# A chunked attention scan and two feed-forward layers on one core: a mask's row of 512 bytes, one raw load moved up, weight pieces fetched between other loads

## The chip, the cores and the metric

The kernel runs on one core of a Trainium2 chip. The metric is the device time of one execution in microseconds (us); the median of three runs of the kernel before is 595.84 us, with 594.42 the lowest and 600.78 the highest.

## The reference

Three layers follow one another on 3072 tokens (4 batches of 768) of 256 features. The first is a linear-recurrence attention with 8 heads, head size 32 and state size 16; the second squares a rectified product; the third multiplies two products. All of it is float32.

```python
def _attn_ref(x, a, B, C):
    log_a = np.log(np.clip(a, 1e-06, 1.0))
    state = np.zeros((batch, H, N, D), dtype=np.float32)
    for c in range(nc):
        xc, Bc, Cc, la = (chunk c of x, B, C, log_a)
        cum = np.cumsum(la, axis=-1)
        L = np.exp(cum[:, :, :, None] - cum[:, :, None, :]) * causal
        CB = np.einsum('bhin,bhjn->bhij', Cc, Bc)
        y_intra = np.einsum('bhij,bhjd->bhid', CB * L, xc)
        y_inter = np.einsum('bhin,bhnd->bhid', Cc, state) * np.exp(cum)[:, :, :, None]
        y[:, :, sl] = y_intra + y_inter
        state = decayed state + np.sum(Bx, axis=2)

def _moe_ref(x, w_in, w_out):        # 256 -> 2048 -> 256
    r = np.maximum(x @ w_in, 0.0)
    return r * r @ w_out

def _moe2_ref(x, w1, w2, w3, w_out): # 256 -> 1024 -> 1024 -> 256
    return ((x @ w1) * (x @ w2) @ w3) @ w_out
```

## The kernel before

**Tiles of tokens and phases.** The tokens go through in six tiles of 512. For a tile, phase A makes `h = x @ w_in` in 16 steps of 128 features (`h_mm`, line 700), rectifies it on ScalarE (line 712), squares it, and adds `g @ w_out` into two PSUM banks (`x2_mm`, line 745). Phase B makes the two products of the third layer in 8 steps (`a_mm` and `b_mm`, line 700 again), multiplies them and adds the product with `w3 @ w_out` into the output (`out_mm`, line 793). Each float32 operand of these products is split in a high and a low part of type fp32r (lines 142 and 139), and three matmuls stand for one product. The order is A0, A1, B0, B1, A2, B2 and so on to B5. `w3 @ w_out` itself is made once (`w3_product`, line 252).

**Attention.** The sequence is cut in chunks of 96 tokens, two of them to a unit. The first six chunks (units 0 to 2) are done in `startup`, ahead of phase A0. The later ones are spread over the phases as numbered slots: `unit_load` fetches a unit's raw B and C (tile `raw`), `unit_split` splits them and writes them to DRAM (`hl_d`), `unit_bc` reads them back in another shape (`bt`, `cb`, twelve small transfers), `unit_e` fetches decay rows (`e`), `chunk_xb` fetches x and B rows (`xb`), and `chunk_g`, `chunk_y` and `chunk_out` compute. Unit 5 is split in a slot of phase A0 (`put(ph, 7, unit_split, 5)`).

**Weights.** They arrive as 512 KB pieces of 8-byte words (tiles `ua`, `uo`, `u`), in an order fixed by `PIECES`: 16 for phase A (`ua0` to `ua15`), then others. `conv_load(n)` issues the next n of them. Each piece is rebuilt as float32 by ScalarE (lines 194, 196, 225) and VectorE (205, 208, 139); one piece goes with each step of phase A0.

**Order.** All transfers are issued by SyncE in the order in which the code is written (`dma` keeps the program's order), one queue, and each waits there for its inputs and for the transfer eight places ahead of it. In `startup` and A0 every engine keeps the written order as well (`in_order`, `held`).

**Addresses.** Tiles are laid out pool by pool. In the built program the weight tiles (pool `wts`) and the tiles `x20` and `x21`, which hold phase B's `x`, begin 320 bytes past a multiple of 512. Then comes `cmask`, 96 floats or 384 bytes in a row. Everything laid out behind it (`xt`, the moving operand of phase A's `h_mm`; `wo2`, in the same place; `tmp`, `gp`, and the attention's tiles) begins 192 past one, except that `xt` of tile 1 lies in the weight pool, at 320. `const` tiles (`bt`, `cb` of most units) begin at 128.

```python
    cmask = act1.tile([P, CH], F32, tag="cmask", name="cmask")
...
        chunk_xb(2)
        conv_load(1)
        for g in range(3, FIRST[1]):
            chunk_xb(g, f"w12{1 + g}")
        conv_load(2)
        unit_load(4)
...
        decays_e_out()
        conv_load(4)
```

Of the kernel before, what the change touches and what calls it, by code (L numbers as in the profile page):

```python
# [7 lines left out]
F32 = mybir.dt.float32  # L8
# [7 lines left out]
P = 128  # L16
# [3 lines left out]
CH = 96  # L20
# [36 lines left out]
def kernel(  # L57
# [102 lines left out]
    def conv_load(n=1):  # L160
        for _ in range(n):
            i = next_load[0]
            if i >= n_conv:
                return
            kind, j = PIECES[i]
            if kind == "3":
                if at_piece[0] <= last_in.get(PLACE[j % 8], -1):
                    return
                last_in[PLACE[j % 8]] = i + 2 - j % 2
                t = wts.tile([P, 512, 2], U32, tag=PLACE[j % 8], name=f"u3{j}")  # L170
                k = N_O + j
            else:
                place = f"w{kind}{j}"
                if at_piece[0] <= last_in.get(place, -1):
                    return
                t = wts.tile([P, 512, 2], U32, tag=place, name=f"u{kind}{j}")
                k = {"a": N_O + N_3, "o": 0, "12": N_O + N_3 + N_A}[kind] + j
            next_load[0] += 1
            dma(out=t, in_=w_in[k].bitcast(U32).rearrange("p (c w) -> p c w", w=2))
            stage[i] = t  # L180
# [88 lines left out]
    cb = const.tile([96, 4, 2, UW], F32R, name="cb")  # L269
    idc = const.tile([P, 4, 32], F32, name="idc")  # L270
    id2 = const.tile([P, 32], F32, name="id2")
    cmask = act1.tile([P, CH], F32, tag="cmask", name="cmask")
    ident = wts.tile([P, P], F32, tag="wa9", name="ident")
    e_d = dram.tile([4, 2, 2, 8, H, CH], F32, name="e_d")
    m_rel = new_tmp()
# [123 lines left out]
    def unit_load(u):  # L399
        gs = UNITS[u]  # L400
        n = len(gs) * CH
        raw = at.tile([P, 2, UW], F32, tag="raw", name="raw")
        b, t = divmod(gs[0] * CH, S)
        t0 = t
        while t < t0 + n:
            k, i = divmod(t, UT)
            m = min(UT - i, t0 + n - t)
            dma(
                out=raw[:, :, t - t0:t - t0 + m],
                in_=raw_in[b * (S // UT) + k].rearrange("p (s t) -> p s t", s=2)[:, :, i:i + m],  # L410
            )
            t += m
        units[u] = {"B": raw[:, 0, :n], "C": raw[:, 1, :n]}
# [56 lines left out]
    def unit_bc(u, places=None):  # L470
        n = len(UNITS[u])
        bu, cu = bt, [cb[:, :, pos] for pos in range(2)]
        units[u]["c2"] = None if places else cb
        if places:
            bu = wts.tile([96, 4, 2, P], F32R, tag=places[0], name="bt")
            cu = [wts.tile([96, 4, UW], F32R, tag=p, name="cb") for p in places[1:]]
            for c in cu:
                nc.gpsimd.memset(c.bitcast(F32), 0.0)
            unit_rows(bu)
        units[u]["bc"] = bu, cu  # L480
        hl = units[u]["hl"].rearrange("l (p r) s t -> l r p s t", p=4)
        for j in range(n):
            for k, part in enumerate((0, 0, 1)):
                dma(out=bu[32 * k:32 * k + 32, :, j, :CH].bitcast(F32), in_=hl[part, :, :, 0, j * CH:(j + 1) * CH])
        for k, part in enumerate((0, 1, 0)):
            for pos in range(2):
                r0 = 32 * k + 16 * pos
                dma(out=cu[pos][r0:r0 + 16, :, :n * CH].bitcast(F32), in_=hl[part, 16 * pos:16 * pos + 16, :, 1, :n * CH])
# [327 lines left out]
    def put(ph, s, f, *args):  # L816
        plan.setdefault((ph, s), []).append(lambda: f(*args))
# [83 lines left out]
    def attention_plan_1():  # L901
        ph = ("A", 0)
        for j, s in enumerate(ASLOT):
            g = FIRST[1] + j
            put(ph, s, chunk_pre, g)
            put(ph, s, chunk_mask, g)
            put(ph, s + 1, chunk_g, g, 0)
            put(ph, s + 1, chunk_g, g, 1)
            put(ph, s + 2, chunk_y, g)
        put(ph, 7, unit_split, 5)  # L910
        put(ph, 10, unit_bc, 5)
        put(ph, 12, unit_e, 5)
        put(ph, ASLOT[0] + 3, chunk_xb, 9)
        put(ph, ASLOT[1] + 3, chunk_xb, 10)
        put(ph, 2, unit_load, 5)

    def startup():
        ys = {}
# [14 lines left out]
        conv_load(1)  # L933
        chunk_xb(1)
        chunk_xb(2)
        conv_load(1)
        for g in range(3, FIRST[1]):
            chunk_xb(g, f"w12{1 + g}")
        conv_load(2)
        unit_load(4)  # L940
        for u in range(3):
            unit_e0(u)
        decays_ln()
# [13 lines left out]
        decays_e(1)  # L957
        unit_pad(2)
        decays_e_out()
        conv_load(4)  # L960
        chunk_pre(0)
        unit_gm(0, 0)
        unit_gm(0, 1)
# [12 lines left out]
        unit_split(3, "w120")  # L976
        unit_rows(bt)
        nc.gpsimd.memset(cb.bitcast(F32), 0.0)
        unit_bc(3)
        chunk_pick(1, 1)  # L980
        chunk_ds(1, ds[1])
# [13 lines left out]
        chunk_out(0, ys[0])  # L995
        chunk_hand(2, ds[2])
        chunk_xb(6)
        chunk_pick(3, 0)
        chunk_m0(2, 1)
        conv_bits(0)  # L1000
# [4 lines left out]
        chunk_m0(3, 0)  # L1005
        chunk_out(1, ys[1])
        unit_split(4, "w121")
        unit_e(3)
        chunk_xb(7)
        chunk_hand(3, ds[3])  # L1010
        chunk_pick(4, 0)
        conv_words(1)
# [11 lines left out]
        chunk_pick(5, 0)  # L1024
        chunk_m0(4, 1)
        chunk_out(3, ys[3])
        unit_bc(4, BCPLACE)
        unit_e(4)
        conv_bits(1)
# [22 lines left out]
    with in_order():  # L1052
        startup()
# [136 lines left out]
```

## Time and profile before

| | |
|---|---|
| median of 3 runs | 595.84 us (594.42 to 600.78) |
| the profiled execution | 599.25 us, of which the profile's span is 597.5 us |
| mean granted TensorE clock | 0.983 of full speed |
| TensorE matmul busy (PE) | 564.8 us, 95% |
| TensorE weight load busy (PEld) | 463.9 us, 78% |
| VectorE (DVE) | 345.4 us, 58% |
| ScalarE (ACT) | 308.1 us, 52% |
| GpSimd (POOL) | 90.5 us, 15% |
| moved by DMA | 60.33 MB, 101 GB/s over the span |

The shares are over the whole span, whose stages differ: the first 126 us hold the startup, the rebuilding of the weights and most of the waits; behind them TensorE has hardly an idle microsecond. The granted clock of a stretch is given as a share of full speed: 1.00 is 2.4 GHz and 0.50 is 1.2 GHz.

### The profile page before, as it was taken

How to read it: one execution, taken by the hardware profiler on the slowest of the kernel's cores; microseconds unless marked ns; L12 is line 12 of the kernel's file. 1: busy time of each engine (PE TensorE's matmuls, PEld its weight loads, DVE VectorE, ACT ScalarE, POOL GpSimd, SP SyncE). 2: the span in 40 equal slices, each digit the busy share in tenths (PEclk: the TensorE clock that was granted, in tenths of full speed). 3: DMA queues.
4: the chain of work that ended last, by engine and by line, in shares of the span. 5: the costliest groups of instructions: out<-in, count | busy, mean ns of one | idle time of the engine just before them, and what ended most of it. 6: DMA issues, size and time to landing. Idle time of an engine off the chain costs nothing.

```text
span 597.5 us, 10302 instructions
## 1 busy us (share of the span) xinstructions
PE 564.8 (95%) x3884; PEld 463.9 (78%) x3884; DVE 345.4 (58%) x613; ACT 308.1 (52%) x640; POOL 90.5 (15%) x149
## 2 busy tenths in 40 slices
PE   5776898899999999999999999999999999999997
PEld 5654676678888888888778888778888778888786
DVE  1677888687879745455646456544456553544332
ACT  4676898687876434353434354353444343534331
POOL 2817110000002313003023004021030030000000
PEclk8899799799999999999999999999999999999999
DMA  8857657124165543046241064230162220100001
GB/s 239 282 136 207 211 217 281 35 79 169 70 210 143 144 101 89 1 132 152 67 110 54 23 159 110 50 86 3 34 180 68 70 50 1 36 1 0 1 1 36
DMA packets 48850, 60.33 MB, mean 101 GB/s; under 512 B 22944, under 2 KB 36640, under 8 KB 48800
## 3 DMA queue, kind: packets, MB, share of 16 engines
q1 hardware_dynamic: 48800, 59.67, 34.3%
q8 instruction: 31, 0.51, 0.4%
q14 instruction: 19, 0.16, 0.1%
HBM read 50.99 MB, written 8.65 MB: 100 GB/s over the span
## 4 chain that ended last, share of the span: by engine, by line
PE 83%; DMA 7%; SPq 4%; DVE 2%; ACT 2%; issue 1%; POOL 0%; POOLq 0%; ACTq 0%; DVEq 0%
PE mm L700 42%; PE acc L745 20%; PE acc L793 12%; PE mm L252 4%; SPq L91 4%; DMA raw<-in_raw_dram 2%; PE y L667 2%; PE g L555 2%; DMA e<-e_d 2%; DMA hl_d<-hl 1%; DMA uo<-in_w_dram 1%; DMA u<-in_w_dram 1%; PE g L576 1%; PE mm L604 1%; PE y L651 1%
## 5 line engine op out<-in xcount | busy, mean ns | idle before, releaser
L745 PE MATMUL acc<-gp,wa 128*128 128x512 f32 x576 | 152.3, 402 | 7.9 <-ACT gp L728 6.7
L700 PE MATMUL mm<-xt,wa 128*128 128x512 f32 x576 | 152.0, 401 | 4.3 <-DVE wa L139 2.1
L728 ACT CAST gp<-tmp 128x512 fp32r<-128x512 f32 x144 | 89.4, 621 | 112.8 <-DVE tmp L784 53.1
L139 DVE TENSOR_TENSOR gp<-tmp,gp 128x512 fp32r<-128x512 f32 x144 | 102.1, 709 | 76.0 <-ACT gp L728 75.8
L700 PE MATMUL mm<-x,w 128*128 128x512 f32 x576 | 143.6, 395 | 0.8 <-ACT x L142 0.4
L745 PEld LDWEIGHTS acc<-gp,wa 128*128 128x128 f32 x576 | 107.2, 190 | 35.1 <-ACT gp L728 8.4
L700 PEld LDWEIGHTS mm<-xt,wa 128*128 128x128 f32 x576 | 106.9, 191 | 30.2 <-DVE wa L139 4.2
L700 PEld LDWEIGHTS mm<-x,w 128*128 128x128 f32 x576 | 104.3, 188 | 22.5 <-ACT x L142 1.1
L712 ACT ACTIVATE tmp<-mm 128x512 f32<-128x512 f32 x96 | 57.3, 597 | 48.4 <-PE mm L700 47.7
L793 PEld LDWEIGHTS acc<-w3o,gp 128*128 128x128 f32 x576 | 75.9, 189 | 4.6
L793 PE MATMUL acc<-w3o,gp 128*128 128x256 f32 x576 | 78.9, 284 | 0.0
L784 DVE TENSOR_TENSOR tmp<-tmp,mm 128x512 f32<-128x512 f32 x48 | 32.8, 683 | 55.8 <-PE mm L700 43.3
L722 DVE TENSOR_TENSOR tmp<-tmp 128x512 f32<-128x512 f32 x64 | 45.0, 703 | 31.5 <-ACT tmp L712 30.9
L776 ACT COPY tmp<-mm 128x512 f32<-128x512 f32 x48 | 27.7, 586 | 42.1 <-PE mm L700 40.9
L493 POOL TENSOR_SCALAR_AFFINE_SELECT e<-e 96x768 f32<-96x768 f32 x26 | 28.2, 1100 | 130.3 <-DMA e<-e_d 115.0
L512 POOL TENSOR_TENSOR xb<-xb,dec 96x256 f32<-96x256 f32 x32 | 22.3, 697 | 120.6 <-DMA xb<-in_xb_dram 113.5
L561 DVE TENSOR_TENSOR e<-g,e 128x384 f32<-128x384 f32 x52 | 27.6, 551 | 16.6 <-PE g L555 9.9
L512 POOL TENSOR_TENSOR pb<-xb,dec 96x128 f32<-96x128 f32 x32 | 15.8, 493 | 84.3 <-PE y L651 84.1
L667 PE MATMUL y<-e,xb 128*32 128x96 f32 x512 | 23.0, 263 | 3.4 <-issue 2.2
L667 PEld LDWEIGHTS y<-e,xb 128*32 128x32 f32 x512 | 13.3, 113 | 15.5 <-issue 12.0
L512 POOL TENSOR_TENSOR pb<-idc,dec 32x128 f32<-32x128 f32 x32 | 15.7, 491 | 56.5 <-PE y L651 54.7
L252 PE MATMUL mm<-wo,w 128*128 128x256 f32 x128 | 23.5, 283 | 0.5 <-DVE w L139 0.3
(90 smaller groups left out, 471.6 us busy)
## 6 DMA issues: line engine op xcount, KB each, us to landing
u<-in_w_dram SPq DMA_DIRECT2D x24, 512.0 KB, 4.1
e<-e_d SPq DMA_DIRECT2D x44, 192.0 KB, 4.3
ua<-in_w_dram SPq DMA_DIRECT2D x16, 512.0 KB, 7.6
xb<-in_xb_dram SPq DMA_DIRECT2D x32, 192.0 KB, 4.0
bt<-hl_d SPq DMA_DIRECT2D x78, 48.0 KB, 2.0
hl_d<-gp SPq DMA_DIRECT2D x9, 384.0 KB, 4.1
cb<-hl_d SPq DMA_DIRECT2D x66, 48.0 KB, 2.0
out_dram<-tmp SPq DMA_DIRECT2D x12, 256.0 KB, 2.2
```

The costliest lines, as they stand in the source:

```text
L139: return nc.vector.tensor_tensor(out=lo, in0=src, in1=hi.bitcast(F32), op=ALU.subtract)
L252: nc.tensor.matmul(acc[:, :DM], v[:, l, e % 4 * P:(e % 4 + 1) * P], wo2[1 + e // 2][r][:, e % 2 * DM:(e % 2 + 1) * DM], start=(n == 0), st ...
L493: nc.gpsimd.affine_select(out=m, in_=m, pattern=[[0, m.shape[1]], [1, CH]], base=0, channel_multiplier=-1, compare_op=ALU.is_ge, fill=0.0,)
L512: nc.gpsimd.tensor_tensor(out=out, in0=v_in, in1=d.to_broadcast([r.stop - r.start, 4, 2, out.shape[3]]), op=ALU.mult)
L667: nc.tensor.matmul(ys[32 * q:32 * q + 32, hg], ch["xb"][:, 32 * h:32 * h + 32], es[g][:, h], start=True, stop=True, skip_group_check=True,)
L700: nc.tensor.matmul(ps, w[m][:, l, col + k * P:col + (k + 1) * P], rhs[k][:, r, :], start=((l, r, k) == (1, 0, 0)), stop=((l, r, k) == (0, ...
L712: nc.scalar.activation(r, ps, AF.Relu)
L722: nc.vector.tensor_tensor(out=g32, in0=r, in1=r, op=ALU.mult)
L728: nc.scalar.copy(g[:, 0, :], d[k])
L745: nc.tensor.matmul(acc["x2", t][e], wa[m][:, l, 256 + e * P:256 + (e + 1) * P], g[:, r, :], start=(m == 0 and n == 0), stop=(m == MF - 1 a ...
L784: nc.vector.tensor_tensor(out=p32, in0=prods[t, m], in1=ps, op=ALU.mult)
L793: nc.tensor.matmul(acc["o"][sub // 2][:, sub % 2, :], g[:, l, sub * P:(sub + 1) * P], w3o[m // 2][:, r, m % 2, :], start=(m == 0 and n == ...
```

## The change

It has three parts. The mask's tile is made 128 floats wide, of which the first 96 are used, so that the tiles behind it move by 128 bytes and begin 320 past a multiple of 512, as the weights do. The raw load of unit 5 leaves slot 2 of phase A0 and is issued in `startup`, behind the writes of the decay rows. The weight pieces 1 to 7, which were issued in `startup` as 1, 2 and 4 at three places, are issued at seven places: behind the early loads, and singly or in pairs between the transfers of units 3 and 4. Together with that, `chunk_xb(7)` is issued ahead of `unit_e(3)`.

```diff
-    cmask = act1.tile([P, CH], F32, tag="cmask", name="cmask")
+    cmask = act1.tile([P, P], F32, tag="cmask", name="cmask")[:, :CH]
...
-        put(ph, 2, unit_load, 5)
...
         chunk_xb(2)
-        conv_load(1)
         for g in range(3, FIRST[1]):
             chunk_xb(g, f"w12{1 + g}")
-        conv_load(2)
         unit_load(4)
+        conv_load(1)
...
         decays_e_out()
-        conv_load(4)
+        conv_load(1)
+        unit_load(5)
...
         nc.gpsimd.memset(cb.bitcast(F32), 0.0)
+        conv_load(1)
         unit_bc(3)
...
         chunk_xb(6)
+        conv_load(1)
...
         unit_split(4, "w121")
+        chunk_xb(7)
+        conv_load(2)
         unit_e(3)
-        chunk_xb(7)
...
+        conv_load(1)
         unit_bc(4, BCPLACE)
```

On SyncE's queue, from the loads of `startup` to unit 3's write (`hl_d3`) and read-back, this stands in a row before; `e_d` are the decay rows, `raw_154` is unit 4's raw load.

```order
L91 DMA ua2_150<-in_w_dram 128x1024
L91 DMA ua3_152<-in_w_dram 128x1024
L91 DMA raw_154<-in_raw_dram 128x2x192
L91 DMA e_d_96<-tmp_178 128x4x96
L91 DMA e_d_96<-tmp_248 128x4x96
L91 DMA ua4_255<-in_w_dram 128x1024
L91 DMA ua5_257<-in_w_dram 128x1024
L91 DMA ua6_259<-in_w_dram 128x1024
L91 DMA ua7_261<-in_w_dram 128x1024
L91 DMA hl_d3_368<-hl_363 128x2x384
L91 DMA bt_90<-hl_d3_368 32x4x96 x6
L91 DMA cb_91<-hl_d3_368 16x4x192 x6
```

And there now:

```order
L91 DMA raw_148<-in_raw_dram 128x2x192
L91 DMA ua1_150<-in_w_dram 128x1024
L91 DMA e_d_96<-tmp_174 128x4x96
L91 DMA e_d_96<-tmp_244 128x4x96
L91 DMA ua2_251<-in_w_dram 128x1024
L91 DMA raw_253<-in_raw_dram 128x2x64
L91 DMA raw_253<-in_raw_dram 128x2x32
L91 DMA hl_d3_361<-hl_356 128x2x384
L91 DMA ua3_366<-in_w_dram 128x1024
L91 DMA bt_90<-hl_d3_361 32x4x96 x6
L91 DMA cb_91<-hl_d3_361 16x4x192 x6
```

Ahead of the write of unit 3 stand three pieces (0, 1 and 2) where eight stood, and unit 5's two raw transfers (`raw_253`) have come in. Further on in the same queue, around the decay rows of unit 4 (`e_683`) and the pieces that phase A0 starts to load, this stood before:

```order
L91 DMA cb_666<-hl_d4_556 16x4x192
L91 DMA e_683<-e_d_96 32x2x768 x4
L91 DMA ua8_764<-in_w_dram 128x1024
L91 DMA ua9_766<-in_w_dram 128x1024
L91 DMA raw_780<-in_raw_dram 128x2x64
L91 DMA raw_780<-in_raw_dram 128x2x32
L91 DMA ua10_792<-in_w_dram 128x1024
```

From unit 3's read-back to unit 4's, this stands there now:

```order
L91 DMA xb_487<-in_xb_dram 96x512
L91 DMA ua4_489<-in_w_dram 128x1024
L91 DMA hl_d4_553<-hl_548 128x2x384
L91 DMA xb_555<-in_xb_dram 96x512
L91 DMA ua5_557<-in_w_dram 128x1024
L91 DMA ua6_559<-in_w_dram 128x1024
L91 DMA e_561<-e_d_96 32x2x768 x4
L91 DMA xb_605<-in_xb_dram 96x512
L91 DMA ua7_665<-in_w_dram 128x1024
L91 DMA bt_667<-hl_d4_553 32x4x96 x6
```

Pieces 4 to 7 have come in here, and behind them unit 4's decay rows are followed by pieces 8 to 12 with no raw load between. The orders of TensorE, VectorE and ScalarE are as before; on GpSimd one mask of chunk 6 stands some instructions later.

## Rows read from the trace of the kernel before

**Rows 1.** The page's first part: busy us, share of the span, instructions.
```profile
PE 564.8 (95%) x3884; PEld 463.9 (78%) x3884; DVE 345.4 (58%) x613; ACT 308.1 (52%) x640; POOL 90.5 (15%) x149
```

**Rows 2.** Busy us by stage: PE, PEld, DVE, ACT, POOL, granted clock, DMA share, GB/s.
```profile
54.00:62.00 8.00, 2.66 (x12) 1.53 (x10) 3.61 (x10) 1.98 (x8) 3.75 (x5) 1.00 1.01 320
62.00:69.00 7.00, 7.00 (x38) 5.06 (x39) 5.74 (x11) 7.00 (x15) 1.14 (x2) 0.52 0.72 225
69.00:100.00 31.00, 30.86 (x197) 24.18 (x196) 26.86 (x47) 28.85 (x64) 4.57 (x7) 1.00 0.68 260
126.00:597.00 471.00, 466.19 (x2801) 387.60 (x2800) 257.06 (x452) 213.34 (x425) 55.31 (x85) 1.00 0.28 77
```

**Rows 3.** ScalarE in order of time, 51 to 64 us: start, us, idle before, releaser.
```profile
51.73 0.67 ACT L194 ACTIVATE cvs<-ua 128x512 f32<-128x512 f32 x1
...
54.27 0.62 ACT L225 CAST wa<-cvs 128x512 fp32r<-128x512 f32 x1
60.92 0.44 ACT L142 CAST gp<-raw 128x96 fp32r<-128x96 f32 x2 [6.02 <-DMA raw<-in_raw_dram]
...
61.79 0.67 ACT L194 ACTIVATE cvs<-ua 128x512 f32<-128x512 f32 x1
```

**Rows 4.** TensorE in order of time, 54 to 62 us.
```profile
55.99 1.67 PE L700 MATMUL mm<-xt,wa 128*128 128x512 f32 x6 [1.06 <-DVE wa L139]
61.93 0.80 PE L745 MATMUL acc<-gp,wa 128*128 128x512 f32 x1 [4.28 <-ACT gp L728]
```

**Rows 5.** SyncE's issues in order of time, 18 to 62 us.
```profile
18.06 2.90 SPq L91 DMA_DIRECT2D ua<-in_w_dram  x4
22.00 0.38 SPq L91 DMA_DIRECT2D hl_d<-hl  x1
30.34 3.40 SPq L91 DMA_DIRECT2D bt<-hl_d  x6
...
52.80 0.89 SPq L91 DMA_DIRECT2D ua<-in_w_dram  x2
53.73 1.38 SPq L91 DMA_DIRECT2D raw<-in_raw_dram  x2
```

**Rows 6.** The chain that ended last, 18 to 62 us: start, us, what.
```profile
22.00 8.32 DMA hl_d<-hl
...
54.34 6.50 DMA raw<-in_raw_dram
```

**Rows 7.** DMA issues from 18 to 21.5 us: KB each, median us to landing.
```profile
ua<-in_w_dram SPq DMA_DIRECT2D x4, 512.0 KB, 8.2
```

**Rows 8.** The chain that ended last, behind 126 us: start, us, what, matmuls.
```profile
129.96 1.37 PE mm L700 x6
...
139.37 1.38 PE mm L700 x6
```

**Rows 9.** The same chain behind 505 us; phase A5 from 517.93, B4 and B5 around it.
```profile
505.26 2.75 PE mm L700 x12
...
517.93 4.20 PE mm L700 x18
522.12 4.20 PE acc L745 x18
...
587.71 5.78 PE acc L793 x48
```

**Rows 10.** TensorE groups by shape, 120 to 597 us: busy us, mean ns of one.
```profile
L745 PE MATMUL acc<-gp,wa 128*128 128x512 f32 x473 | 122.6, 397 | 1.2 <-DVE gp L139 1.2
...
L793 PE MATMUL acc<-w3o,gp 128*128 128x256 f32 x576 | 78.9, 284 | 0.0
L252 PE MATMUL mm<-wo,w 128*128 128x256 f32 x120 | 22.0, 282 | 0.3 <-DVE w L139 0.3
L252 PE MATMUL mm<-wo2l,w 128*128 128x256 f32 x60 | 16.9, 282 | 0.0
```

**Rows 11.** The same view, 200 to 597 us: the `xt` matmuls of phases A2 to A5.
```profile
L700 PE MATMUL mm<-xt,wa 128*128 128x512 f32 x384 | 99.5, 395 | 0.0
```

## The prediction

> **What bounds the kernel now.** The page's first part comes first: TensorE's matmuls are busy for 564.8 of 597.5 us [rows 1]. That alone says little, since matmuls overlap, so the next view is the table of busy time by stage [rows 2]. From 126 us to the end TensorE is busy in 466.19 of 471 us, and ScalarE and VectorE in about half of them: there the time is the number of matmuls by the distance from one to the next, and nothing but a shorter distance saves anything. Ahead of that, from 62 to 100 us, ScalarE (35.85 of 38 us) and TensorE (37.86 of 38) are both full, because each step of phase A0 rebuilds a weight piece on ScalarE. A hole in this stretch moves all that follows it. There is one: between 54 and 62 us TensorE works for 2.66 us and ScalarE for 1.98.
>
> The engines' timelines show what the hole is. ScalarE ends a piece at 54.89 (54.27 + 0.62), and its next instruction, unit 5's split, waits 6.02 us for the tile `raw` [rows 3]. The cast of `gp` stands behind it, and TensorE, which needs that `gp`, stays idle for 4.28 us up to 61.93 [rows 4]. SyncE issued the raw load at 53.73 [rows 5] and the second of its two transfers took 6.50 us [rows 6], at a DMA share of 1.01 with weight pieces in front. Right behind the hole the granted clock is 0.52 over 7 us [rows 2], the lower level of 1.2 GHz for nearly all of it, after 4.28 idle microseconds at the upper level of 2.4 GHz.
>
> **The raw load moved up.** It goes from behind piece 9 to behind piece 2. The work that it feeds stays at its place. By the new order ahead of it stand the early loads, three pieces, and the decay rows; where the queue was fullest a piece landed 8.2 us after its issue [rows 7]. At its new place it is issued well before the 18.06 us at which piece 4 was issued [rows 5], so it lands by some 26 us and is wanted at 54.89. The 6.02 us of ScalarE go.
>
> What is late next? I followed ScalarE's order past the split. Two casts and the `gp` cast take it to about 55.8, and then it wants piece 8 (line 194, at 61.79 before, 0.87 us behind the split [rows 3]). Piece 8 was issued at 52.80 and stood just ahead of the raw load, which landed at 60.84. Would piece 8 alone have held the engine up? With the old queue, by about as long as its landing passes 55.8, so the reordering of the queue decides.
>
> **Weight pieces between other loads.** The bytes are the same; only places change. Before, four pieces were issued at 18.06 to 20.96, and the write of unit 3 (`hl_d`) behind them took 8.32 us from 22.00 [rows 5, 6]. Its read-back, 12 small transfers that SyncE issues one by one, started only at 30.34, and everything behind it on that in-order queue stood. Now the write has no such four in front. I estimate it at 2 to 4 us, an end at about 24 us, and 6 us won for the queue. Pieces 4 to 7 come back in behind it: four issues of 0.44 us (0.89 for two in [rows 5]), or 1.8 us, and their bytes take part of the old slack. So piece 8 is issued some 4 us earlier, at about 48.8, and lands some 6.5 us later, as long as the raw load took behind the same queue [rows 6], at 55.3. That is when ScalarE wants it. Pieces 4 to 7 have room: the last, piece 7, is wanted by line 194 at 51.73 [rows 3]. At the worst landing time shown, 8.2 us, it must be issued by 43.5. The read-back's first six issues took 3.40 us [rows 5], so all twelve end at about 31, and eleven more of about 0.45 us put piece 7 at 36.
>
> So the worth of both moves together lies between TensorE's hole of 4.28 us and ScalarE's of 6.02. More than ScalarE's is possible only by 0.6, since ScalarE is full on both sides. TensorE is full behind the hole as well, but 7 us of that ran at a granted clock of 0.52 [rows 2], and without the hole I expect 1.00, as ahead of it. That can shorten TensorE's own path by up to 3.4 us, half of the 7, on top of its 4.28, and leaves ScalarE the limit. I take 5.4 us, the middle of 4.3 and 6.6. It lies wholly on the path: from 62 to 126 us the same engines do the same work earlier, the later loads hang on TensorE's and VectorE's progress and move along, and behind 126 us there is no gap to swallow it.
>
> **The mask's row.** It adds no instruction; one tile grows by 128 bytes. What it moves is where the operands begin. The trace holds both cases. Phase A5's `h_mm` reads `xt` at 192 against weights at 320: 18 matmuls in 4.20 us, 233.3 ns each; `x2_mm` with `gp` at 192 takes the same [rows 9]. Phase B's `x` lies at 320 like its weights: 12 in 2.75 us, 229.2 ns [rows 9]. The nearest control is phase A1, with the same weight tiles as A5 but its `xt` in the weight pool, at 320: six in 1.37 and 1.38 us, 228 to 230 ns [rows 8]. So like beginnings go with a distance shorter by 3 to 4 ns, and I take 4.1.
>
> Where it counts: 473 `x2_mm` matmuls behind 120 us [rows 10] and 384 `h_mm` ones of A2 to A5 [rows 11], together 857; times 4.1 ns this is 3.5 us. The 256-column matmuls also mix beginnings now: 576 of `out_mm`, whose stationary `gp` is at 192, and 180 of line 252 [rows 10], at 120.4 ns (48 in 5.78 us [rows 9]). No row shows them with like beginnings. From zero to the whole 4.1 ns they give 0 to 3.1 us; a loss is not excluded, and with the sign turned it would be as large. I take half, as for half the columns: 756 times 2.05 ns, 1.5 us. Ahead of 120 us ScalarE sets the pace, and the shorter distance is hidden.
>
> The Trainium skill's page "SBUF — State Buffer", section "Who interferes with whom", speaks against this part: it gives TensorE two independent read ports, one for the moving operand and one for the weight load, and says that TensorE never waits on anyone. By that, where two operands begin could not matter, this term would be zero and the sum only the first one; the rows of A1 and A5 disagree with it by 3 to 4 ns a matmul.
>
> **Sum.** 5.4 + 3.5 + 1.5 = 10.4 us. On the profiled execution of 599.25 us that gives 588.8. That execution is 3.4 us above the median, inside the spread of the three runs, so I take the difference to the median: 595.84 - 10.4 = 585.4 us, 1.7% faster. Within 1% of the median (5.96 us) this kernel's measurement can hardly be told from no change.
>
> **The rivals.**
> 1. *Alignment is worth nothing.* The 3 to 4 ns would come from which tiles are read, not from where they begin. For it: no tile is seen at both places in the same use. Against it: A1 and A5 have the same weights and the same three passes. Time: 595.84 - 5.4 = 590.4. The page's rule above gives just this time.
> 2. *The hole is filled by the next late load.* If the write of unit 3 is not much quicker, piece 8 lands at 60 us and ScalarE waits for it instead of for `raw`, for 4 to 5 us; or a piece among 4 to 7 is late by as much. For it: piece 8 was issued directly ahead of the raw load and the queue is in order. Against it: four pieces leave its front. What remains is the alignment: 595.84 - 5.0 = 590.8.
> 3. *Like beginnings are the dear case.* If operands that begin alike met in the memory in the uses that no row shows, or `xt` in its new place did, each of the 857 + 756 matmuls would lose what I count as a gain: 1613 times 4.1 ns, 6.6 us. With the hole gone that is 1.2 us slower, 597.0; with rival 2 as well, 602. It decides from 3.4 ns on, where 1613 matmuls eat up the 5.4 us. Against it: both kinds of row with like beginnings are the quicker ones.
> 4. *Nothing arrives*: rival 1 and rival 2 together, 595.8.
>
> **How the numbers follow.** The forecast has a chance of 0.50, rival 1 0.17, rival 2 0.18, rival 3 0.07, rival 4 0.08. The predicted time is the forecast's, 585.4. The range: low end from 6.6 us for the hole and 3.5 + 3.1 us for alignment, 595.84 - 13.2 = 582.6, less the 1.4 us by which the lowest of the three runs lies under the median, 581.2. The high end takes in rivals 1 and 2 and ends at 591.5; left out are rivals 3 and 4 and the tails. Faster by over 1% (589.9 or less) is nearly all of the forecast and a third of rivals 1 and 2, which lie at the bound: 0.61. Slower by over 1% is rival 3 with rival 2, and late pieces that I did not foresee: 0.06. The rest, 0.33, is within 1%.
>
> **What the changed profile would show.** The split of unit 5 follows line 225 on ScalarE with no wait, and TensorE's idle time of 4.28 us near 58 us is gone or under 1 us. The granted clock stays at 1.00 from 54 to 69 us. Unit 3's write takes under 4 us. Phase A5's runs of 18 read 4.13 us or so, and 48 of `out_mm` 5.7. If ScalarE waits there for `ua` instead, rival 2 holds; if runs of 18 still read 4.20, rival 1; if they read more, rival 3. A second low-clock stretch earlier than 62 us would mean that pieces 4 to 7 come late. The prediction is wrong above all if piece 8 lands after 57 us.

## The result and the profile after

The changed kernel takes 592.43 us, the median of 20 runs (588.86 to 598.69). The kernel before, run beside it, takes 597.5 us (20 runs, 594.42 to 603.97). The ratio is 0.990 with a 95% interval of 0.987 to 0.993. It is formed from the undisturbed executions alone, so it isn't quite the quotient of the two medians. The forecast was 585.4 us with a range of 581.2 to 591.5: the kernel is faster, but by 1.0% and not by 1.7%, and the time lies 0.9 us above the range. The base moved as well: the forecast was taken off a median of 595.84 from three runs, and 20 runs give 597.5.

The profiled execution after has a span of 592.0 us, 5.5 less than before. Its stages, to be read against [rows 2] (PE, PEld, DVE, ACT, POOL, granted clock, DMA share, GB/s):

```profile
54.00:62.00 8.00, 4.96 (x41) 3.50 (x42) 3.58 (x10) 3.71 (x8) 2.14 (x4) 0.93 0.98 346
62.00:69.00 7.00, 7.00 (x24) 5.71 (x24) 6.88 (x14) 7.00 (x16) 1.86 (x2) 0.59 0.64 201
```

The hole is smaller, but it is there: between 54 and 62 us TensorE is busy for 4.96 us, and behind it the granted clock is again near its lower level of 1.2 GHz (0.59, before 0.52). ScalarE in order of time answers to [rows 3]:

```profile
52.84 0.44 ACT L142 CAST gp<-raw 128x96 fp32r<-128x96 f32 x2
53.19 0.61 ACT L728 CAST gp<-tmp 128x512 fp32r<-128x512 f32 x1
58.28 0.66 ACT L194 ACTIVATE cvs<-ua 128x512 f32<-128x512 f32 x1 [4.49 <-DMA ua<-in_w_dram]
```

The split of unit 5 has no wait, as forecast. Two instructions later ScalarE waits 4.49 us for piece 8. TensorE's stop, to be read against [rows 4], went from 4.28 us to 3.04. A `gp` cast of line 728 releases it again, but the next one in order, at 60.89; the cast that ended the stop before now runs at 53.19, ahead of the wait.

```profile
61.56 2.08 PE L745 MATMUL acc<-gp,wa 128*128 128x512 f32 x4 [3.04 <-ACT gp L728]
```

SyncE's issues say when piece 8 was asked for. The row at 52.80 begins with it, and answers to the one of the same start in [rows 5]:

```profile
20.13 0.37 SPq L91 DMA_DIRECT2D hl_d<-hl  x1
...
22.84 3.77 SPq L91 DMA_DIRECT2D bt<-hl_d  x6
...
40.91 6.39 SPq L91 DMA_DIRECT2D bt<-hl_d  x6
47.40 3.46 SPq L91 DMA_DIRECT2D cb<-hl_d  x6
50.97 1.77 SPq L91 DMA_DIRECT2D e<-e_d  x4
52.80 2.83 SPq L91 DMA_DIRECT2D ua<-in_w_dram  x5
```

Unit 3's write is issued at 20.13 and its read-back begins at 22.84 (before 22.00 and 30.34), so the queue did win 7.5 us. Unit 4's read-back begins at 40.91, where it began at 42.01, and piece 8 is issued at 52.80 in both. The first two of its twelve transfers go out at 40.91 and 43.94, each 0.02 us behind the landing of the piece eight places ahead (pieces 5 and 6, at 40.89 and 43.92). The chain that ended last shows what took the rest of the 7.5 us (start, us, what):

```profile
38.59 10.03 DMA ua<-in_w_dram
...
48.69 0.30 SPq L91
...
52.80 5.46 DMA ua<-in_w_dram
58.28 0.66 ACT cvs L194
```

Before, the same chain had decay rows at this place, landed at 47.29:

```profile
40.52 6.77 DMA e<-e_d
```

The piece issued at 38.59 is piece 7, for which the forecast had 36. It landed at 48.62, and SyncE's next issue in the chain follows 0.07 us later. By the queue's rule that each transfer waits for the one eight places ahead, that issue is the second `cb` of unit 4: behind piece 7 come six `bt` and one `cb`.

The alignment shows in phase A5, the runs of [rows 9] (and 36 matmuls of `w3_product`, which serve below as a mark of time):

```profile
127.50 4.31 PE mm L252 x36
...
513.66 4.11 PE mm L700 x18
517.76 4.08 PE acc L745 x18
...
582.16 5.76 PE acc L793 x48
```

Eighteen matmuls of 512 columns take 4.11 and 4.08 us where they took 4.20, so 228.3 and 226.7 ns each where it was 233.3. The 48 of 256 columns take 5.76 where they took 5.78: nothing. One new wait came up in phase B0. TensorE after, and below it the same place before:

```profile
201.45 0.39 PE L700 MATMUL mm<-x,w 128*128 128x512 f32 x1
203.56 0.66 PE L555 MATMUL g<-cb,bt 96*128 96x192 f32 x4 [1.72 <-DMA cb<-hl_d]
204.07 4.28 PE L700 MATMUL mm<-x,w 128*128 128x512 f32 x11
208.18 1.36 PE L793 MATMUL acc<-w3o,gp 128*128 128x256 f32 x10
```

```profile
205.76 0.39 PE L700 MATMUL mm<-x,w 128*128 128x512 f32 x1
...
206.72 2.73 PE L700 MATMUL mm<-x,w 128*128 128x512 f32 x11
209.29 1.37 PE L793 MATMUL acc<-w3o,gp 128*128 128x256 f32 x10
```

TensorE comes there 4.31 us sooner than before and leaves only 1.11 sooner: a wait of 1.72 us for a read-back that isn't there yet, then eleven matmuls at the lower clock, 4.28 us for 2.73. Where the 5.5 us of this execution arose, from the rows shown and those of before:

| mark on TensorE | before | after | gain so far |
|---|---|---|---|
| 36 matmuls of line 252, A1 | 131.33 | 127.50 | 3.83 |
| ahead of `cb`'s wait, B0 | 205.76 | 201.45 | 4.31 |
| ten matmuls of line 793 behind it | 209.29 | 208.18 | 1.11 |
| first run of 18, A5 | 517.93 | 513.66 | 4.27 |
| 48 matmuls of line 793, B5 | 587.71 | 582.16 | 5.55 |

### The profile page after: what moved, and what is told of

It is laid out like the page before. It is cut to its first block, busy times and chain, and to the rows that moved or that the text cites. A ratio compares the mean times of both kernels' runs of the same rounds, so it can differ in the third digit from the quotient of the medians.

```text
span 592.0 us, 10298 instructions
## 1 busy us (share of the span) xinstructions
PE 561.4 (95%) x3884; PEld 466.0 (79%) x3884; DVE 344.5 (58%) x613; ACT 307.5 (52%) x640; POOL 89.9 (15%) x149
## 4 chain that ended last, share of the span: by engine, by line
PE 82%; DMA 7%; ACT 4%; DVE 2%; SPq 2%; issue 1%; POOL 1%; POOLq 0%; ACTq 0%; DVEq 0%
PE mm L700 41%; PE acc L745 19%; PE acc L793 11%; PE mm L252 4%; DMA ua<-in_w_dram 3%; SPq L91 2%; PE y L667 2%; PE g L555 2%; DMA uo<-in_w_dram 1%; PE mm L604 1%; DMA xb<-in_xb_dram 1%; DMA raw<-in_raw_dram 1%; DMA e<-e_d 1%; PE g L576 1%; ACT gp L728 1%
## 5 line engine op out<-in xcount | busy, mean ns | idle before, releaser
L745 PE MATMUL acc<-gp,wa 128*128 128x512 f32 x576 | 149.1, 397 | 6.9 <-ACT gp L728 5.5
L700 PEld LDWEIGHTS mm<-x,w 128*128 128x128 f32 x576 | 105.5, 190 | 22.8 <-ACT x L142 1.1
```

What stands on the lines that cost most here:

```text
L700: nc.tensor.matmul(ps, w[m][:, l, col + k * P:col + (k + 1) * P], rhs[k][:, r, :], start=((l, r, k) == (1, 0, 0)), stop=((l, r, k) == (0, ...
L745: nc.tensor.matmul(acc["x2", t][e], wa[m][:, l, 256 + e * P:256 + (e + 1) * P], g[:, r, :], start=(m == 0 and n == 0), stop=(m == MF - 1 a ...
```

## The experiments

Theory: the change pulled the raw load out of the hole, but piece 8 takes its place since it is issued no sooner, and the alignment is worth its full 5 us. The rival is that the alignment gives less and the hole more, or that the loss near 204 us is the main one. Times are medians; every ratio is against the kernel before on the same chip in the same session.

**The mask alone** (the kernel before with the first hunk of the change), in two sessions.

```diff
-    cmask = act1.tile([P, CH], F32, tag="cmask", name="cmask")
+    cmask = act1.tile([P, P], F32, tag="cmask", name="cmask")[:, :CH]
```

> The kernel before with the mask's row of 512 bytes alone; no load is moved. Theory: the operands' beginnings shorten 857 matmuls of 512 columns by 4 to 6 ns each and leave those of 256 columns alone. Expected: phase A5's runs of 18 read about 4.1 us where 4.20 stood, 48 of out_mm still 5.8, ScalarE still waits 6.0 us for raw, and the time falls by 3.5 to 5 us (ratio 0.992 to 0.994). Rival: the shorter distance in the changed kernel comes from something else (another layout of the weight tiles): then the runs of 18 stay at 4.20 and the time stays.

> The kernel before with the mask's row of 512 bytes and nothing else, once more, beside the changed kernel. It gave 0.9906 of before on another chip; by the rows of phase A5, 857 matmuls of 512 columns at 5.3 ns less are 4.5 us, which is 0.9925. A ratio of 0.990 to 0.993 agrees with that term, one of 0.986 or less would mean that the mask does more than shorten these matmuls.

Measured: 595.52 us and 0.9906 (0.987 to 0.994); in the second session 595.36 us and 0.9932 (0.990 to 0.997). Both executions show runs of 18 at 4.11 and 4.08 us in A5 and 48 in 5.76, and ScalarE's wait for `raw` is still there (4.9 us in the first, 5.8 in the second). So the mask is worth 4 to 6 us. By its rows, 36 matmuls of A5 went from 8.40 to 8.19 us, 5.8 ns each, and 857 times 5.8 ns is 5.0 us.

**The loads alone** (the changed kernel with the mask's row back at 384 bytes).

```diff
-    cmask = act1.tile([P, P], F32, tag="cmask", name="cmask")[:, :CH]
+    cmask = act1.tile([P, CH], F32, tag="cmask", name="cmask")
```

> The changed kernel with the mask's row of 384 bytes again, so that both moves of loads remain. Theory: ScalarE's 6.0 us for raw become about 4.5 us for weight piece 8, the startup ends about 2 us sooner, and the end of the stage of the weights (126 us) comes about 3.5 us sooner; some of that is given back near 204 us, where TensorE comes to unit 13's read-back before it has landed. Expected: 2 to 3.5 us less than before (ratio 0.994 to 0.997). Rival: the moves are worth 5.4 us as forecast and the mask is worth little: ratio 0.991.

Measured: 596.78 us, ratio 0.9917 (0.988 to 0.995). ScalarE waits 4.5 us for `ua`, and runs of 18 are back at 4.20. The 36 matmuls of line 252 start at 126.18, 5.15 us sooner than before. The time is nearer to the rival's 0.991 than to the theory's 0.994 to 0.997, though the interval reaches both: by this run the moved loads are worth about 5 us by themselves, in spite of the wait for piece 8.

**The raw load alone** (the kernel before, with unit 5's raw load ahead of the four pieces).

```diff
-        conv_load(4)
+        unit_load(5)
+        conv_load(4)
...
-        put(ph, 2, unit_load, 5)
```

> The kernel before with unit 5's raw load alone moved up, ahead of pieces 4 to 7. Theory: the hole is shared by two late loads, and raw was only 1.9 us later than piece 8 (60.84 against 58.91); ScalarE then waits 3 to 4 us for piece 8, and the time falls by at most 2 us (ratio 0.997 or more). Rival: raw alone is the cause: the hole goes and 4 to 6 us are saved (0.990 to 0.993).

Measured: 598.86 us, ratio 0.9972 (0.993 to 1.001), no difference that can be told. ScalarE in this kernel:

```profile
57.29 0.45 ACT L142 CAST gp<-raw 128x96 fp32r<-128x96 f32 x2
...
61.54 0.69 ACT L194 ACTIVATE cvs<-ua 128x512 f32<-128x512 f32 x1 [3.29 <-DMA ua<-in_w_dram]
```

With the queue as it was before, the wait for `raw` goes and 3.29 us of wait for piece 8 come two instructions later. This is the second rival of the prediction by itself: the raw load and piece 8 stood side by side, and either alone keeps the hole.

**The pieces without the raw load** (the changed kernel with unit 5's raw load back in slot 2 of A0).

```diff
-        unit_load(5)
...
+        put(ph, 2, unit_load, 5)
```

> The changed kernel with the raw load of unit 5 back in slot 2 of phase A0. Theory: the raw load and piece 8 stand for the same 4 to 5 us behind one queue, so either of them alone keeps the hole; with the raw load back, the split waits for raw for 4 to 6 us (it is issued behind piece 9, at 53 us or so) and the time is that of the changed kernel within 1.5 us. Rival: the pieces that were moved have freed the queue by enough, raw lands by 57 us and the wait is under 2 us; then the time is 2 us or more below the changed kernel.

Measured: 595.56 us, ratio 0.9957 (0.992 to 1.000), 2.8 us above the changed kernel beside it (592.74 us), so by the time neither answer fits: the theory had said within 1.5. By the trace the theory holds. ScalarE waits for `raw`, longer than before:

```profile
58.91 0.45 ACT L142 CAST gp<-raw 128x96 fp32r<-128x96 f32 x2 [6.45 <-DMA raw<-in_raw_dram]
```

It waits behind piece 9 again, and TensorE stops for 4.9 us where the changed kernel stops for 2.9. The two moves need one another.

**Piece 8 ahead of unit 4's read-back** (one more piece at the last of the new places).

```diff
-        conv_load(1)
+        conv_load(2)
         unit_bc(4, BCPLACE)
```

> The changed kernel with weight piece 8 issued next to piece 7, ahead of unit 4's read-back and decay rows. Theory: piece 8's place in the queue is what ScalarE waits for at 54 us. With the piece there by 50 us, the 4.5 us on ScalarE and the 3.0 us on TensorE go, and so does the low clock behind them; the stage of the weights ends 3 to 4.5 us sooner than in the changed kernel, of which some may be lost again near 204 us. Expected: 2 to 4 us less than the changed kernel, ratio to the kernel before 0.983 to 0.987. Rival: the queue as a whole is too slow and ScalarE waits as long for piece 9: no gain over the changed kernel (0.990).

Measured: 590.68 us, ratio 0.9828 (0.978 to 0.988). On SyncE (first fence) pieces 7 and 8 are issued at 37.51 and 38.67; on ScalarE (second fence) the piece that was waited for is taken at 54.34 without a wait:

```profile
37.51 1.51 SPq L91 DMA_DIRECT2D ua<-in_w_dram  x2
41.80 4.01 SPq L91 DMA_DIRECT2D bt<-hl_d  x6
```

```profile
54.34 0.67 ACT L194 ACTIVATE cvs<-ua 128x512 f32<-128x512 f32 x1
...
58.58 0.68 ACT L194 ACTIVATE cvs<-ua 128x512 f32<-128x512 f32 x1 [0.98 <-DMA ua<-in_w_dram]
```

What is left of the hole is 0.98 us for piece 9, and the stretch from 62 to 69 us runs at a granted clock of 1.00. The 36 matmuls of line 252 start at 123.47, 7.9 us sooner than before and 4.0 sooner than in the first trace of the changed kernel. That is what the forecast took for the change itself. Some of it is lost again: TensorE waits 2.33 us for `cb` at 200.47, and eleven matmuls behind it take 4.17 us. The ratio is formed beside other executions of the kernel before than those of the changed kernel, and the intervals overlap, so the trace shows the hole gone more surely than the median shows its worth.

**Pieces 5 and 6 behind the decay rows.** Is it the order of these bytes, or the waits eight places on, that keeps unit 4's read-back late?

```diff
         chunk_xb(7)
-        conv_load(2)
         unit_e(3)
+        conv_load(2)
```

> The changed kernel with pieces 5 and 6 issued behind unit 3's decay rows instead of ahead of them. Theory A: unit 4's read-back is paced by the landings of the pieces that stand among the eight transfers ahead of its own, so it starts sooner (the first wait is then on decay rows), but ends within 1 us of 50.9 us, and piece 8 is issued at 52 to 53.5 as in the changed kernel; ScalarE's wait for ua stays at 4 to 5 us and the time within 1.5 us. Rival B: the pieces ahead of the decay rows take the rate away from them; then the read-back ends 2 us or more sooner, piece 8 is issued by 50.5, the wait shrinks to 2.5 us or less, and the time is 2 us lower. Rival C: pieces 5 and 6 come too late for phase A0, and ScalarE waits for them at 44 to 50 us.

Measured: 593.89 us, ratio 0.9892 (0.985 to 0.993), against 590.24 of the changed kernel beside it; the intervals overlap. On SyncE:

```profile
38.99 6.10 SPq L91 DMA_DIRECT2D bt<-hl_d  x6
45.32 4.69 SPq L91 DMA_DIRECT2D cb<-hl_d  x6
...
51.95 2.82 SPq L91 DMA_DIRECT2D ua<-in_w_dram  x5
```

The read-back begins 1.9 us sooner than in the first trace of the changed kernel, takes 11.0 us instead of 10.0, and ends at 50.01, 0.9 us sooner. Piece 8 is issued at 51.95, and ScalarE still waits 3.5 us. Theory A holds as far as this goes: whatever starts the read-back, the landings among the eight transfers ahead end it at about the same time, and rival B's end of 2 us or more sooner didn't come. Two of theory A's numbers were missed: the wait is shorter than its 4 to 5 us, and the time is 3.65 us above the changed kernel, not within 1.5. Rival C's late pieces don't explain that (ScalarE's longest wait for a piece between 40 and 50 us is 0.27); what does was not tried.

**The changed kernel again**, twice, as the base of its neighbours.

> The changed kernel again, as the base of the three kernels beside it, on one chip. The mask alone gave 0.9906 and the loads alone 0.9917; if the two parts simply add, the whole change is at 0.982 of before. If they get in each other's way, it stays at 0.990, as it was measured first. In the trace: the split of unit 5 without a wait, 4 to 5 us of ScalarE's wait for ua at line 194 near 58 us, and 1.5 to 2 us of TensorE's wait for cb near 204 us.

> The changed kernel once more, beside the kernel with the mask alone on the same chip. Pooled over two earlier sessions it is at 0.989 of before. If the moved loads are worth something on top of the mask, it is 2 us or more below the kernel with the mask alone; if what they win near 58 us is given back near 204 us and in other waits, the two are within 1.5 us of each other.

Measured: 592.74 us and 0.9878 (0.983 to 0.993); 590.24 us and 0.9869 (0.983 to 0.991), here 5.1 us below the mask alone beside it. So the moved loads are worth something on top of the mask, and the two parts don't cancel: the first expectation, 0.982 for plain addition, was too good, but 0.990 was not the last word either. The waits for `ua` are 4.2 and 5.0 us. TensorE's wait for `cb` near 204 us is 1.8 us in the first, with the low clock behind it, and in the second:

```profile
201.44 0.66 PE L555 MATMUL g<-cb,bt 96*128 96x192 f32 x4 [1.00 <-DMA cb<-hl_d]
201.94 2.72 PE L700 MATMUL mm<-x,w 128*128 128x512 f32 x11
```

Here the clock stays up, and the span is 588.5 us. The mask alone has a wait at this place too, 2.60 us in its first trace and 0.65 in its second. So the loss near 204 us is a matter of the single execution, between 1 and 3 us, and not a fixed part of the change.

**The decay rows of phase B0 behind the write.** In the slot that issues unit 13's decay rows:

```diff
-        put0(11, unit_e, u0 + 1)
+        put0(14 if t == 2 else 11, unit_e, u0 + 1)
```

> The changed kernel with one slot altered: in phase B0 the decay rows of the second unit are issued behind the split's write instead of ahead of it. Theory A: the wait for cb near 204 us (1.7 us) and the low clock behind it (204.2 to 207.6 us) come from the write of the high and low parts landing late behind these decay rows; then the wait goes, and the kernel is 2 to 3.5 us faster than the changed kernel beside it. Rival B: the read-back comes late for another reason (the twelve small transfers one by one); then the wait stays at 1.5 us or more and the time is within 1 us. Rival C: the wait goes, but the decay rows, now later, hold VectorE's masks up and TensorE waits for them in its place, time within 1 us.

Measured: 591.92 us, ratio 0.9867 (0.982 to 0.992). TensorE at this place:

```profile
201.26 0.44 PE L555 MATMUL g<-cb,bt 96*128 96x192 f32 x2 [0.25 <-issue]
...
202.00 2.93 PE L700 MATMUL mm<-x,w 128*128 128x512 f32 x12
```

The wait for `cb` is gone and the clock stays up, here and in the next kernel, while all three traces of the changed kernel have it. The write landed 3.4 us after its issue (188.00 to 191.37) where it took 5.8 in the first trace of the changed kernel (190.59 to 196.40), as theory A says. But two of the kernels with pads below, with the decay rows in their old place, don't wait either, so that this place alone makes the wait is likely and not shown. The time is 0.8 us below the changed kernel beside it, less than two medians of six runs can tell: the 2 to 3.5 us are not shown. In this execution a wait of 1.4 us for `e` turns up in phase B4.

**Both repairs together**, piece 8 up and the decay rows behind the write.

> The changed kernel with piece 8 ahead of unit 4's read-back and, in phase B0, the decay rows behind the split's write. If the hole near 58 us and the wait near 204 us are the two places where the gain of the change is lost, the two repairs add: 2 to 4 us for the first (0.9828 against 0.990 of before, measured apart) and 2 to 3.5 us for the second, together 0.975 to 0.981 of before. If the second wait only comes later because the work ahead of it ends sooner, it is back at another place and the time is that of the first repair alone, 0.983.

Measured: 588.92 us, ratio 0.983 (0.978 to 0.988), 3.8 us below the changed kernel beside it and the lowest median of the kernels timed more than once, though not to be told from piece 8 alone (0.9828); the 0.975 to 0.981 expected of two repairs that add didn't come. The 36 matmuls of line 252 start at 122.94, and there is no wait for `cb`. ScalarE still waits 2.38 us for piece 9 at 58.41.

**Where operands begin.** Five builds of the changed loads move the operands. In three the mask lies in the weight pool and a pad of 256, 64 or 192 bytes a row stands in its place ahead of `xt`, `tmp` and `gp`. In two a pad ahead of the weights moves everything: by 128 bytes with the mask's row of 384, and by 64 with that of 512. The first of the five:

```diff
-    cmask = act1.tile([P, P], F32, tag="cmask", name="cmask")[:, :CH]
+    cmask = wts.tile([P, CH], F32, tag="w127", name="cmask")
+    act1.tile([P, 64], F32, tag="pad", name="pad")
```

> The changed kernel with the mask in the weight pool and a pad of 256 bytes a row in its place, so that the operands that begin alike with the weights in the changed kernel (320 past a multiple of 512) begin at 64, half a row of 512 off. In the kernel before they were off by 128. Theory A: only the same beginning modulo 512 helps; then phase A5's runs of 18 read 4.19 to 4.20 us as before, and the time is 3 to 5 us above the changed kernel. Rival B: the beginning counts modulo 256; then they read 4.08 to 4.11 and the time is that of the changed kernel. Rival C: it counts which tiles share a bank of some larger size, not the beginning; then they read something else, over 4.20 or in between.

> The changed kernel with the mask in the weight pool and a pad of 64 bytes a row in its place: xt, tmp, gp and the attention's tiles begin at 384 modulo 512, which is 128 modulo 256, against 64 modulo 256 of the weights. Theory A: stationary and moving operand must begin alike modulo 256; then phase A5's runs of 18 read 4.19 to 4.20 us. Rival B: the beginning at 192 modulo 256 is slow by itself, whatever the weights' beginning; then they read 4.08 to 4.11 us here.

> The changed kernel with the mask's row back at 384 bytes and a pad of 128 bytes ahead of the weights, so that weights and phase B's x begin at 448 (192 modulo 256) and xt, tmp and gp at 320 (64 modulo 256). Theory A: operands that begin 128 bytes apart modulo 256 are slow; then phase A5's runs of 18 read 4.20 us, as in the kernel before, and phase B's twelve matmuls stay at 2.75. Rival B: a moving operand that begins at 192 modulo 256 is slow by itself; then A5's runs read 4.11 and phase B's twelve go up to 2.80. If it is the stationary operand that must not begin there, both are slow.

> The changed kernel with a pad of 64 bytes ahead of the weights: all operands begin alike, at 384 modulo 512 (128 modulo 256). In the kernel with xt, tmp and gp alone at 384, 48 matmuls of 256 columns came to 116 ns each instead of 119.7, and 18 of 512 columns to 4.12 us. If the stationary operand's beginning at a multiple of 128 is what makes the 256-column matmuls shorter, they stay at 116 here (5.6 us for 48), and the x matmuls of phase B, whose weights are now there as well, may gain as much, 2.71 us for twelve in place of 2.75; if it was the distance of 64 between the two operands, 48 are back at 5.76.

> The changed kernel with the mask in the weight pool and a pad of 192 bytes a row in its place: xt, tmp and gp begin at 0 modulo 512, the weights at 320. If a beginning at a multiple of 128 is good for gp as a stationary operand, 48 matmuls of 256 columns take 5.6 us as with 384; if it was the distance of 64 modulo 256, a distance of 192 should show something else. Runs of 18 in phase A5 read 4.11 to 4.13 if only 192 modulo 256 is slow for a moving operand.

The rows are of the chain that ended last, at the end of phase B4 and in A5; where a pad adds a line, lines 700, 745 and 793 are 701, 746 and 794. The pads of 256, of 64 and of 192 bytes:

```profile
511.50 1.43 PE acc L794 x12
512.93 4.11 PE mm L701 x18
517.04 4.08 PE acc L746 x18
```

```profile
507.09 1.39 PE acc L794 x12
508.48 4.12 PE mm L701 x18
512.60 4.12 PE acc L746 x18
```

```profile
509.62 1.41 PE acc L794 x12
511.03 4.20 PE mm L701 x18
515.24 4.20 PE acc L746 x18
```

Everything moved by 128 bytes with the short mask, and by 64 with the long one:

```profile
503.80 2.75 PE mm L701 x12
...
515.03 1.44 PE acc L794 x12
516.47 4.20 PE mm L701 x18
520.67 4.20 PE acc L746 x18
```

```profile
510.82 1.43 PE acc L794 x12
512.25 4.11 PE mm L701 x18
516.36 4.08 PE acc L746 x18
```

All seven arrangements, with the beginnings modulo 512. "Apart" is the beginning of `xt` and `gp` less that of the weights, so 64 and 192 differ in which of the two begins 64 bytes past the other:

| `xt`, `gp` | weights | apart modulo 256 | 18 of line 700, 18 of line 745, A5 | 12 of line 793, B4 |
|---|---|---|---|---|
| 320 (the change) | 320 | 0 | 4.11, 4.08 us | 1.43 us |
| 64 | 320 | 0 | 4.11, 4.08 | 1.43 |
| 384 | 384 | 0 | 4.11, 4.08 | 1.43 |
| 384 | 320 | 64 | 4.12, 4.12 | 1.39 |
| 192 (before) | 320 | 128 | 4.20, 4.20 | 1.44 |
| 320 | 448 | 128 | 4.20, 4.20 | 1.44 |
| 0 | 320 | 192 | 4.20, 4.20 | 1.41 |

The forecast's rule, alike modulo 512, falls with the second row: 256 bytes apart is as good. A place that is slow by itself falls with the sixth, since `xt` at 320 is quick beside weights at 320 and slow beside weights at 448, while phase B's `x`, moved to 448 together with its weights, keeps its 2.75 us for twelve. "Alike modulo 256" falls with the fourth: 64 apart is nearly as good. What the seven rows bear out is that the distance between the two operands modulo 256, with its sign, decides; why, none of them shows, and no distance between these four was tried. The 256-column matmuls, whose stationary operand is `gp`, follow another rule: in B4's runs of twelve they are quickest at 64 and at 192 apart, by some 3.5 and 2 ns each (in B5's runs of 48 by some 2 ns at both, 5.67 and 5.66 us), and the change, from 128 to 0, gives them nothing. The pad of 256 bytes was also timed: 591.36 us, ratio 0.9883 (0.983 to 0.993), the changed kernel's time. Of the other four there is one execution each, which says nothing on a difference of 1 or 2 us.

## Why the prediction was wrong, by its steps

**Where it failed.** "So piece 8 is issued some 4 us earlier, at about 48.8, and lands ... at 55.3." It was issued at 52.80 and landed at 58.26, past the 57 us that the prediction had named as the sign of being wrong; before, the landing was at 58.91. The half of the step on unit 3 was right, the gain even a little low: its write was forecast at 2 to 4 us and its read-back to end at about 31; they took 2.7 us and ended at 30.25 (26.66 + 3.59), 7.5 us won. What failed is the half on what comes back in. Pieces 4 to 7 were charged with the 1.8 us of their issues, "and their bytes take part of the old slack". But piece 7 took 10.03 us to land, and unit 4's read-back may not go on until it has landed, being eight places behind. The rule of eight places stands in the description of the kernel; I applied it to no transfer. Nor were the 8.2 us taken as the worst landing the worst: they are a median [rows 7], and the slowest of those four pieces took 8.7. So piece 7 took over, almost to the tenth, the part that the decay rows had played before: SyncE was free again at 48.62 in place of 47.29, and the decay rows of unit 4 and piece 8 went out at 50.97 and 52.80 in both kernels. That the two times agree to 0.01 us is chance; with pieces 5 and 6 elsewhere it was 51.95, in the two further traces of the changed kernel 53.50 and 52.09. That the place of piece 8 keeps the hole is shown by moving it alone: the wait goes, and the low clock from 62 to 69 us with it. What this is worth in the end is less sure: the ratio of 0.983 (0.978 to 0.988) overlaps with those of the changed kernel.

**The second rival came true in its effect**: ScalarE waits 4 to 5 us for piece 8. Its condition did not, since it asked for a slow write of unit 3. It was priced at 590.8, or 5.0 us under its base, and the two medians of 20 runs lie 5.1 apart. That nearness is luck: the rival gave the loads nothing, and they gave some microseconds, part of which was lost again in phase B0.

**The loads' term.** Forecast 5.4. At the 36 matmuls of line 252 the three traces of the changed kernel are 3.8, 4.2 and 5.2 us ahead, the mask alone 0.2 and 0.6, and the loads alone 5.2, so the loads gave 3.2 to 5.2 by the execution. In the first trace the rows say where it comes from. ScalarE takes piece 8 at 58.28, 3.5 us sooner than the 61.79 before. It is now released by piece 8, landed at 58.26, and no longer by the raw load, landed at 60.84 (2.6 us); and the split and the cast behind it, 0.87 us [rows 3], run ahead of the wait. Phase A0 also begins sooner (ScalarE's first line 712 at 37.55, before at 39.49), but as long as ScalarE waits for piece 8 this only makes the wait longer. With piece 8 up as well it counts: there the first line 712 stands at 38.10, 1.4 us sooner, the 6.02 us of wait are gone, and the mark is 7.9 us ahead. So the 5.4 was, if anything, low for a hole that is really closed. Which wait of the startup lets phase A0 begin sooner was not tried.

**The alignment's terms.** The sum was right and both parts were wrong. The 512-column matmuls gave 5.8 ns each in A5 and not 4.1, 5.0 us for 857 and not 3.5: I took the 228 to 230 ns of phase A1 [rows 8] for the new distance, and A5 came to 226.7 to 228.3. The table's last and third marks say the same: 5.55 less 1.11 is 4.44 us for the 768 such matmuls of A2 to A5, 5.8 ns each. The 256-column ones gave 0.02 us on 48 where 1.5 us in all was forecast. Rivals 1 and 3 fall by the runs of 18 alone. The Trainium skill's page "SBUF — State Buffer", section "Who interferes with whom", from which rival 1's time followed as well, gives TensorE two independent read ports and says that it never waits on anyone. The prediction drew from it that the beginnings could not matter. The runs disagree: with the same instructions and only a pad of 192 or 256 bytes between the tiles, a run of 18 takes 4.20 or 4.11 us.

**What I did not foresee.** Phase B0's read-back of `cb`. The prediction said that behind 126 us "there is no gap to swallow it". There was none in that trace: the read-back landed at 206.13 and TensorE was free for it at 206.15, just in time. In the first trace of the changed kernel it landed at 203.47 and TensorE was free at 201.84: 1.72 us of wait and 1.55 more for eleven matmuls at the lower clock (4.28 for 2.73) are 3.3, of which the table above shows 3.2. That TensorE comes sooner doesn't make the wait by itself, since the read-back moves with it: the kernels with pads of 64 and 192 bytes, with the same loads moved, are free at 200.57 and 199.60 and don't wait, while the mask alone, in its second trace, is free at 205.10 and waits 0.65. In both kernels with the decay rows behind the write the wait is gone; with the rows ahead of it, it shows in all but those two of the traces other than that of the kernel before. Why it is there in one execution and not in another stays open, and so does how much of it is in the median: three traces of the changed kernel have 1.72, 1.75 and 1.00 us of wait, and the kernel without it has a median only 0.8 us lower, too little to be told.

**The base.** Part of the miss in us is the median of three runs: 595.84 against 597.5 from 20 runs, and 598.0, 599.54 and 601.39 in later sessions. The ratios of the changed kernel, 0.990, 0.9878 and 0.9869, are against the first three of these and are gains of 6 to 8 us, where 10.4 were forecast.

## What to carry to other kernels

A transfer that is moved in an in-order queue also moves the waits that count places in it: list, for each transfer behind it, which one it will now wait for, and how long that one takes to land among its new neighbours. When a wait is taken away, look at the next user of the same queue before counting the gain; here piece 8 stood one place from the raw load, and moving one without the other was worth nothing that could be told (0.997, with an interval up to 1.001). And read a distance between matmuls for every pair of places that occurs: a pad of some bytes in an unrelated tile was worth 0.7 to 0.9%, as much as all moved loads.

## What the runs showed of the hardware

The distance from one 512-column fp32r matmul to the next depends on how far past the stationary operand the moving one begins, modulo 256 bytes: 226.7 to 229.2 ns at 0 and 64 (18 in 4.08 to 4.12 us, twelve of phase B in 2.75), 233.3 at 128 and 192 (18 in 4.20). With 256 columns, by how far past the moving operand the stationary one begins, it is 119 to 120 ns at 0 and 128, 117.5 at 192 and 116 at 64 in B4's runs of twelve (1.39 us for twelve at 64), and 120 at 0 and 128 and 118 at 192 and 64 in B5's runs of 48.

A 512 KB piece landed 5.46 us after its issue at 52.80 and 10.03 us after its issue at 38.59, where two pieces, four transfers of decay rows and one of x and B rows, none of them landed, stood ahead of it. TensorE's clock fell from the upper level to the lower after an idle 3.04 us (0.59 from 62 to 69 us) and after one of 1.72 (eleven matmuls in 4.28 us), and stayed up after one of 1.00 at the same place in another execution (2.72 us). It also stayed up there after an idle 2.45 us, in the kernel with everything moved by 128 bytes and the short mask (eleven in 2.73 us), so in these runs the length of a stop alone doesn't tell.
